# Last group finished on VectorE with stores from two queues, 1/std through ScalarE's Ln and Exp, a first load in two parts, and one slot's turnings in pairs

## The chip, the cores and the metric

The kernel runs on one core of a Trainium2 chip. The metric is the device time of one execution in microseconds (us). Five engines run side by side, each in the order of its own queue: TensorE (PE; its weight loads are PEld), VectorE (DVE), ScalarE (ACT), GpSimd (POOL) and SyncE (SP), which here only issues DMA transfers. ScalarE can issue transfers too. They wait for each other through semaphores.

## The reference

Attention over 8 batches, 8 heads, 576 tokens and 64 features a head, in which only scores within tau of a row's maximum count; then a layer norm and a two-layer network on the 512 features, added to its input.

```python
scores = scale * np.matmul(q, k.transpose(0, 1, 3, 2))
thresh = np.max(scores, axis=-1, keepdims=True) - tau
scores = np.where(scores >= thresh, scores, -1000000000.0)
scores = scores - np.max(scores, axis=-1, keepdims=True)
attn = np.exp(scores)
attn = attn / (np.sum(attn, axis=-1, keepdims=True) + 1e-09)
x = np.matmul(attn, v)            # heads side by side: (8, 576, 512)
mu = np.mean(x, axis=-1, keepdims=True)
var = np.mean((x - mu) ** 2, axis=-1, keepdims=True)
xn = (x - mu) / np.sqrt(var + 1e-06) * g_ln
ch = np.maximum(xn @ w_ch1, 0.0) @ w_ch2
return (x + ch).astype(np.float32)
```

All numbers are float32, apart from the network's weights, which arrive as 64-bit floats and are converted in the kernel. The norm's gain g_ln is multiplied into the first weights, and the division by the standard deviation is put off until after the second layer.

## The kernel before

**Attention in slots.** Each batch takes nine slots (SLOTS); a slot treats 256 query rows of two heads, or, in the fifth slot of a batch, the rows that are left of all heads. One loop over the 72 slots writes out the order of all instructions by hand: the program fixes each engine's queue, nothing is reordered later. In a slot TensorE makes the scores (`scores`, L408), VectorE their negated maximum (L422), GpSimd the threshold (L426), ScalarE the exponentials (L436), VectorE the masked weights and their sum (L443). In batch 0 the weights are turned by TensorE against diagonal matrices of 1/sum (`turn_weights`: four turnings `tp`, each copied out of PSUM by ScalarE at L493 or L487, and a rest `tr`); in later batches they go through VectorE transposes and a trip to DRAM (`turn_blocks`). `values_of` multiplies them by v.

**When a turning runs.** `at_quarter(n, i, fn)` puts a call off to place i of slot n. The places -3 to -1 come before the slot's exponentials are issued, the place 0 between the exponentials of the first and of the second two blocks, 1 to 3 later. For the four steps of `turn_weights` the main loop names four places in the next slot (L1090). In the first five slots these are (-1, -1, 0, 0), in the next three (-1, -1, -1, -1), in the ninth (-1, 0, 1, 2).

**The network in groups.** Sixteen groups of 288 tokens follow behind the attention, their matmuls poured between those of the slots by `second_part`. A group starts with the mean over features (`mean_of`, a matmul) and the centring on VectorE (L666, `centre`), then the first layer (`first_part`, tile p, relu at L795 on ScalarE). Within it ScalarE squares the centred input, TensorE sums it to var, ScalarE adds eps (L811), and VectorE makes 1/std in `root`: a first guess by integer arithmetic (L727) and three Newton rounds of three instructions (L731, L734, L735). Mean, var, p, the turnings and the second layer's sums take turns in two PSUM buffers of the pool ps_ff; a new tile waits until the last reader of the old one is done.

**The second layer** of groups 1 to 15 (`second_quarters`) multiplies in seven segments of quarter size (tile seg). ScalarE copies each segment's sum out of PSUM (L880); additions on VectorE and GpSimd combine them to y. `later` queues such calls, which the main loop takes out bit by bit (`drip`). `finish` (L892 and the addition L884) multiplies by 1/std and adds x, on GpSimd; "hi" is the upper half of the features (chunks m = 2 and 3), "done11" and "done12" are the lower half in two parts. `store` transposes a chunk on VectorE (L709) and `send` writes it with four transfers (L716), all issued by SP. A chunk's four transfers hold 32 features each.

**The head.** The queries and keys of the first head pair are loaded with four transfers each (`load_qk`), q issued by SP, k by ScalarE. A transfer is issued only when an earlier one that had the same semaphore has landed, so the order on these queues counts. `turn` scales q on GpSimd (L356) and transposes k and q on VectorE (L359, L368, L369). Meanwhile `constants(22)` keeps TensorE busy with 22 products of constants (88 matmuls; tile warm). ScalarE's function table is loaded where its first exponential stands.

Of the kernel before, what the change touches and what calls it, by code (L numbers as in the profile page):

```python
# [10 lines left out]
I32 = mybir.dt.int32  # L11
# [7 lines left out]
def kernel(  # L19
# [83 lines left out]
    def load_qk(u, engines=(nc.sync, nc.sync), room=None):  # L103


        b, hp = units[u]
        tiles = []
        for i, (name, src) in enumerate((("q", q), ("k", k))):
            if room is None:
                t = ins.tile([128, NB, 32], F32, tag=name, bufs=1, name=f"{name}_in")  # L110
            else:
                t = room[:, i * S : i * S + S].rearrange("p (n c) -> p n c", c=32)
            for h in range(2):
                for e in range(2):
                    g = 2 * h + e
                    engines[i].dma_start(
                        out=t[32 * g : 32 * g + 32],
                        in_=src[b, 2 * hp + h, :, 32 * e : 32 * e + 32].rearrange(
                            "(r n) c -> r n c" if i and b else "(n r) c -> r n c", r=32
                        ),  # L120
                    )
            tiles.append(t)
        loaded[u] = tuple(tiles)

    def load_v(u):
        b, hp = units[u]
        vt = ins.tile([128, 2, J, D], F32, tag="v", name="v_in")
        vr = v_rest[hp]
        both = v[b, 2 * hp : 2 * hp + 2]
        if b:  # L130
            nc.sync.dma_start(
                out=vt.rearrange("p h c d -> p h (c d)"),
                in_=both[:, : J * 128].rearrange("h (p c) d -> p h (c d)", c=J),
            )
        for h in range(0 if b else 2):
            nc.sync.dma_start(
                out=vt[:, h], in_=both[h, : J * 128].rearrange("(c p) d -> p c d", p=128)
            )
        for j in range(2):
            nc.sync.dma_start(  # L140
                out=vr[64 * j : 64 * j + 64, j], in_=both[:, J * 128 :].rearrange("h p d -> p h d")
            )
        values_in[u] = (vt, vr)
# [9 lines left out]
    for t in v_rest:  # L153
        nc.gpsimd.memset(t, 0.0)
    load_v(0)
    make_identity(nc, ident)
    nc.vector.memset(eps_sb, 1e-6)
    nc.vector.memset(avg_sb, 1.0 / DM)
# [186 lines left out]
    def turn(u):  # L345

        q_in, k_in = loaded.pop(u)
        qT = att.tile([128, 2, QH], F32, tag="qT", bufs=4, name="qT")
        kT = att.tile([128, S], F32, tag="kT", bufs=4, name="kT")
        ql = q_last[u % HP]
        nc.gpsimd.tensor_scalar(  # L356
            out=q_in, in0=q_in, scalar1=scl_sb, scalar2=1.0, op0=ALU.mult, op1=ALU.mult
        )
        nc.vector.transpose(kT, k_in.rearrange("p n c -> p (n c)"))  # L359
        for s in range(2):  # L360
            part = q_in[:, 9 * s : 9 * s + 8]
            if by_blocks(u):
                nc.vector.transpose(
                    qT[:, s].rearrange("p (j a c) -> p a j c", j=2, a=4),
                    part.rearrange("p (a j) c -> p a j c", j=2),
                )
            else:
                nc.vector.transpose(qT[:, s], part.rearrange("p n c -> p (n c)"))  # L368
        nc.vector.transpose(  # L369
            ql.rearrange("p (t c) -> p t c", t=2),  # L370
            q_in.rearrange("p (t n) c -> p t n c", t=2)[:, :, 8],
        )
        turned[u] = (qT, kT, ql)
# [338 lines left out]
    def send(g, m, ot):  # L712
        b, t = divmod(g, 2)
        for i in range(4):
            f = m * 128 + 32 * i
            nc.sync.dma_start(  # L716
                out=out[b, t * TOK : (t + 1) * TOK, f : f + 32].rearrange(
                    "(n r) c -> r n c", r=32
                ),
                in_=ot[32 * i : 32 * i + 32].rearrange("p (n c) -> p n c", c=32),  # L720
            )

    def root(y, x, t, step=0):


        if step == 0:
            nc.vector.tensor_scalar(  # L727
                out=y.bitcast(I32), in0=x.bitcast(I32), scalar1=-0.5, scalar2=float(0x5F3759DF),
                op0=ALU.mult, op1=ALU.add,
            )  # L730
        nc.vector.scalar_tensor_tensor(  # L731
            out=t, in0=y, scalar=-0.5, in1=y, op0=ALU.mult, op1=ALU.mult
        )
        nc.vector.tensor_mul(t, t, x)  # L734
        nc.vector.scalar_tensor_tensor(out=y, in0=t, scalar=1.5, in1=y, op0=ALU.add, op1=ALU.mult)  # L735
        if step == 0:
            root(y, x, t, 1)
        elif step == 1:
            aside.append(lambda: root(y, x, t, 2))
        else:  # L740
            rooted.append(y)

    rooted = []
    HT, HD, HM = TOK // 2, ND // 2, NK // 2
# [30 lines left out]
    def first_part(g):  # L775


        xc = centred.pop(g)
        rb = sq = None
        plain = g == 0  # L780
        sums_of = differences() if g == 1 else iter(())
        for d in range(ND):
            while conversion.ended < 4 * (d // 4 + 1):
                yield 0, 0
            while d == ND - 2 and len(rooted) <= g:
                run_all(aside)
            p1 = ps_ff.tile([128, TOK], F32, tag="ff", name="p1")
            for c in range(NK):
                product(
                    p1, lhsT=w1_sb[c][:, d * 128 : (d + 1) * 128], rhs=xc[:, c],  # L790
                    start=(c == 0), stop=(c == NK - 1),
                )
                if c < NK - 1:
                    yield 1, 1
            nc.scalar.activation(hidden[:, d], p1, func=AF.Relu)  # L795
            next(sums_of, None)
            yield 2, 1
            if sq is None and d and (plain or part > 1 or d == ND // 2 - 1):
                squared = d
                sq = hidden[:, ND - NK :]  # L800
                nc.scalar.activation(sq, xc, func=AF.Square)
                for c in range(1, NK):
                    nc.gpsimd.tensor_tensor(out=sq[:, 0], in0=sq[:, 0], in1=sq[:, c], op=ALU.add)
            elif sq is not None and rb is None and (
                d >= squared + (7 if plain else 3) and part > (0 if plain else 1)
                or d == ND - NK - 1
            ):
                var = ps_ff.tile([128, TOK], F32, tag="ff", name="var")
                product(var, lhsT=avg_sb, rhs=sq[:, 0], start=True, stop=True)
                rb = ffn.tile([128, TOK], F32, tag="rb", bufs=2, name="rb")  # L810
                nc.scalar.activation(sq[:, 2], var, func=AF.Identity, bias=eps_sb)  # L811
                aside.append(lambda: root(rb, sq[:, 2], sq[:, 3]))
                yield 1, 1
        for _ in sums_of:
            pass
        return rb
# [18 lines left out]
    def second_quarters(g, rb):  # L835
# [13 lines left out]
        def later(*calls, urgent=None):  # L849
            for what, cost, fn, eng, *args in calls:  # L850

                def go(what=what, fn=fn, eng=eng, args=args):
                    fn(eng, *args)
                    done.add(what)

                drops.append((urgent, now, eng, cost, go))
# [29 lines left out]
        def finish(eng, i, j=None):  # L886
# [6 lines left out]
            add(eng, z, z, x)  # L893

        dve, pool = nc.vector, nc.gpsimd
        later(("t3", 3, by_fours, pool, b12, b22, b12, ALU.subtract), urgent=pool)
        banks_taken[0] = True
        yield from segment(w2[0, 0], b11, y11)
# [21 lines left out]
        later(  # L920
            ("u4", 1, add, dve, y12, y21, p5), ("u3", 1, add, dve, y21, y21, p7),
            ("22", 1, add, dve, y22, y21, p5), ("21", 1, add, dve, y21, y21, p4),
            ("hi", 3, finish, pool, 1),
        )
        yield 2, 0.5
        last = segment(s4, b22)
        for _ in range(12):
# [2 lines left out]
        while waiting_mean:  # L930
            mean_of(waiting_mean.pop(0))
        p3 = yield from last
        later(("12", 1, add, dve, y12, y12, p3), ("done12", 2, finish, pool, 0, 1))
        later(*((f"o{m}", 1, store, dve, g, m, y[:, m]) for m in (2, 3, 0, 1)))
        yield 2, 0.5

    def ffn_steps(g):
# [99 lines left out]
    for n in range(NS):  # L1037
# [46 lines left out]
        if blocks_go:  # L1084
            scr = turn_blocks(s, es)
            at_quarter(n + 1, 0, lambda s=s, scr=scr, box=box: box.append(fetch(s, scr)))
        else:

            made = turn_weights(s, es, diags)
            for i, at in enumerate(  # L1090
                (-1, -1, 0, 0) if s <= HP else (-1, -1, -1, -1) if s < 2 * HP else (-1, 0, 1, 2)
            ):
                if i < 3:
                    at_quarter(n + 1, at, next, made)
                else:
                    at_quarter(n + 1, at, lambda made=made, box=box: box.append(next(made)))
# [62 lines left out]
```

## Time and profile before

| what | value |
|---|---|
| median of 3 runs (lowest to highest) | 1367.26 us (1367.08 to 1368.72) |
| the profiled execution | 1367.01 us |
| its span, first to last instruction | 1365.0 us |
| granted TensorE clock | 0.997 |
| TensorE busy, share of the span | 97% |
| VectorE, ScalarE, GpSimd busy | 68%, 33%, 45% |
| first matmul; first scores; last matmul ends | 2.36; 10.17; 1352.7 us |
| last store issued; span ends | 1362.2; 1365.0 us |

A line of a timeline has start and length in us, engine, line of the kernel, operation, the tile it writes and those it reads, and in brackets how long the engine stood idle before it and what it waited for. "x4" means that four instructions are drawn together. In lists of waits the numbers are us in total, how many times, and the longest. "SPq" is a queue that issues transfers. TensorE's matmuls overlap, so its busy time shows that it has work, not how fast it is; the waits show where it has none.

### The profile page before, as it was taken

To read this page: it belongs to the slowest core of one execution; us is meant where nothing else is said; L and a number is where in the kernel's file an instruction comes from. 1 tells how busy PE (TensorE), PEld (TensorE's weight loads), DVE (VectorE), ACT (ScalarE), POOL (GpSimd) and SP (SyncE) were. 2 spreads that over 40 slices of the span, in tenths; PEclk is the share of its full clock that TensorE was granted. 3 is DMA by queue.
4 is the path that set the end of the run, shared out by engine and by line. 5 is a ranking of instruction groups with operands and counts; after the bars stand their busy time and mean duration, and the time that the engine had idled before them with its cause. 6 is when DMAs were issued, how large, how long until landed. Compare 5 with 4: busy or idle time off the path is not lost.

```text
span 1365.0 us, 40999 instructions
## 1 busy us (share of the span) xinstructions
PE 1330.1 (97%) x17648; PEld 1007.4 (74%) x17648; DVE 921.5 (68%) x1638; ACT 455.3 (33%) x991; POOL 616.7 (45%) x823
## 2 busy tenths in 40 slices
PE   8989999999999999999999999999999999999996
PEld 7766666868677686867778696877869687786966
DVE  6988967776765777676776767657776767666211
ACT  4866532232322323232333323233232223333120
POOL 3554445444534444444534554443444445344313
PEclk9999999999999999999999999999999999999998
DMA  9822475357644666437744476446754476444201
GB/s 170 248 66 88 105 198 156 140 166 196 187 149 145 183 175 193 150 119 191 203 136 162 137 202 176 149 145 187 200 167 149 138 180 179 145 151 143 53 16 18
DMA packets 322020, 206.88 MB, mean 152 GB/s; under 512 B 247984, under 2 KB 279472, under 8 KB 313776
## 3 DMA queue, kind: packets, MB, share of 16 engines
q1 hardware_dynamic: 317072, 203.68, 51.9%
q8 instruction: 138, 2.26, 0.7%
q10 hardware_dynamic: 4736, 0.59, 0.4%
q14 instruction: 42, 0.34, 0.1%
q0 software_dynamic: 32, 0.00, 0.0%
HBM read 120.46 MB, written 83.76 MB: 150 GB/s over the span
## 4 chain that ended last, share of the span: by engine, by line
PE 88%; DVE 4%; ACT 3%; POOL 1%; issue 1%; DMA 0%; POOLq 0%; DVEq 0%; ACTq 0%; SPq 0%
PE p L101 35%; PE seg L101 31%; PE sc L408 10%; PE sc L591 8%; PE sc L601 2%; PE tp L101 1%; DVE e L443 1%; ACT e L436 1%; DVE w L298 1%; PE var L101 0%; PE mean L101 0%; DMA x_room<-in_moe_w_ch_dram 0%; DVE neg L422 0%; DVE et L533 0%; DVE w L275 0%
## 5 line engine op out<-in xcount | busy, mean ns | idle before, releaser
L101 PE MATMUL p<-xc,w 128*64 128x288 f32 x4096 | 518.2, 408 | 13.0 <-ACT hidden L795 5.0
L101 PEld LDWEIGHTS p<-xc,w 128*64 128x64 f32 x4096 | 288.3, 137 | 220.6 <-issue 15.2
L422 DVE TENSOR_REDUCE neg<-sc 128x2 f32<-128x1152 f32 x144 | 188.7, 1351 | 242.5 <-PE sc L408 241.9
L459 POOL TENSOR_SCALAR e<-e,den 128x576 f32<-128x576 f32 x252 | 193.4, 779 | 134.6 <-DVE den L448 134.6
L101 PE MATMUL seg<-hidden,w 128*64 128x144 f32 x3840 | 247.9, 287 | 0.0
L101 PEld LDWEIGHTS seg<-hidden,w 128*64 128x64 f32 x3840 | 234.9, 137 | 11.5 <-issue 8.5
L443 DVE SCALAR_TENSOR_TENSOR e<-sc,thr,e 128x576 f32<-128x576 f32 x288 | 222.2, 810 | 17.9 <-POOL thr L426 11.6
L795 ACT ACTIVATE hidden<-p 128x288 f32<-128x288 f32 x256 | 106.3, 416 | 323.3 <-PE p L101 323.2
L426 POOL TENSOR_SCALAR thr<-neg,low_sb 128x2 f32<-128x2 f32 x144 | 41.5, 288 | 377.5 <-DVE neg L422 377.4
L436 ACT ACTIVATE e<-sc,neg 128x576 f32<-128x576 f32 x288 | 197.6, 754 | 4.1 <-DVE neg L422 4.1
L533 DVE STREAM_TRANSPOSE et<-e 128x1152 f32<-128x1152 f32 x112 | 153.3, 1374 | 14.3 <-POOL e L459 13.7
L408 PE MATMUL sc<-kT,qT 64*64 64x384 f32 (+3 forms) x2048 | 139.5, 404 | 1.9 <-DVE e L443 1.7
L591 PE MATMUL sc<-em,v_in 128*64 128x128 f32 (+1 forms) x2368 | 129.5, 263 | 0.0
L591 PEld LDWEIGHTS sc<-em,v_in 128*64 128x64 f32 x2368 | 122.8, 137 | 7.9
L101 PE MATMUL seg<-hidden,stage 128*64 128x144 f32 x1920 | 123.3, 287 | 0.0
L101 PEld LDWEIGHTS seg<-hidden,stage 128*64 128x64 f32 x1920 | 117.6, 137 | 2.9 <-issue 2.9
L614 ACT COPY x<-sc 128x128 f32<-128x128 f32 x120 | 31.6, 265 | 242.0 <-PE sc L408 171.5
L865 POOL TENSOR_TENSOR hidden<-hidden 128x576 f32<-128x576 f32 x60 | 84.8, 1427 | 51.9 <-ACT hidden L795 42.3
L408 PEld LDWEIGHTS sc<-kT,qT 64*64 64x64 f32 x2048 | 76.3, 133 | 42.6 <-issue 21.0
L880 ACT COPY part<-seg 128x288 f32<-128x288 f32 x75 | 30.2, 403 | 194.2 <-PE seg L101 190.2
L865 DVE TENSOR_TENSOR hidden<-hidden 128x576 f32<-128x576 f32 x60 | 51.2, 887 | 49.1 <-PE seg L101 46.1
L101 PE MATMUL seg<-hidden,e 128*64 128x144 f32 x960 | 65.3, 286 | 0.0
(140 smaller groups left out, 1140.1 us busy)
## 6 DMA issues: line engine op xcount, KB each, us to landing
scr<-et SPq DMA_DIRECT2D x63, 1152.0 KB, 4.9
em<-scr SPq DMA_DIRECT2D x63, 1024.0 KB, 5.8
out_dram<-ot SPq DMA_DIRECT2D x256, 36.0 KB, 3.7
q_in<-in_q_dram SPq DMA_DIRECT2D x124, 72.0 KB, 2.7
k_in<-in_k_dram SPq DMA_DIRECT2D x120, 72.0 KB, 3.0
er<-scr SPq DMA_DIRECT2D x126, 64.0 KB, 5.2
v_in<-in_v_dram SPq DMA_DIRECT2D x28, 256.0 KB, 5.5
w<-in_moe_w_ch_dram SPq DMA_DIRECT2D x12, 512.0 KB, 5.0
```

The source lines that it names most:

```text
L101: nc.tensor.matmul(out[r], lhsT=lhsT[:, r], rhs=rhs, **flags)
L408: nc.tensor.matmul(sc[h][64 * i : 64 * i + 64, at : at + n], lhsT=ql[r] if s == HP else qT[r, half, j * 128 + 64 * i : j * 128 + 64 * i + 64],
L422: nc.vector.tensor_reduce(out=neg[:, i], in_=pairs[h], axis=AXL.X, op=ALU.max, negate=True,)
L426: nc.gpsimd.tensor_scalar(out=thr[:, i], in0=neg[:, i], scalar1=-1.0, scalar2=low_sb, op0=ALU.mult, op1=ALU.add,)
L436: nc.scalar.activation(es[:, i], blocks[i], func=AF.Exp, bias=neg[:, i : i + 1])
L443: nc.vector.scalar_tensor_tensor(out=es[:, i], in0=blocks[i], scalar=thr[:, i : i + 1], in1=es[:, i], op0=ALU.is_ge, op1=ALU.mult, accum_o ...
L459: nc.gpsimd.tensor_scalar(out=es[:, i], in0=es[:, i], scalar1=den[:, i : i + 1], scalar2=1.0, op0=ALU.mult, op1=ALU.mult,)
L533: nc.vector.transpose(et[:, :, 64 * h : 64 * h + 64].rearrange("p n (j c) -> p j n c", j=2), es[:, 2 * h : 2 * h + 2].rearrange("p j (n c) ...
L591: nc.tensor.matmul(dst[64 * h : 64 * h + 64], lhsT=vt[:, h, c, :], rhs=pick(em[:, 2 * j : 2 * j + 2, c], h), start=c == 0 and first, stop= ...
L614: nc.scalar.copy(x_of(2 * b + (s > HP))[:, s % (HP + 1), 128 * j : 128 * j + 128], pv[j])
L795: nc.scalar.activation(hidden[:, d], p1, func=AF.Relu)
L865: eng.tensor_tensor(out=out[at], in0=in0[at], in1=in1[at], op=op)
```

## The change

The change has four parts.

In the **last group** `finish` runs on VectorE for "hi" and "done12"; the stores of chunks 2 and 3 are queued right behind "hi" instead of behind "done12", and the second and fourth transfer of each chunk are issued by ScalarE.

**1/std**: ScalarE takes the logarithm of var + eps and exp(-0.5 times it), and VectorE makes one Newton round in place of the guess and three rounds. A table set that holds both functions is named ahead of the first activation.

**The first q** is loaded in two parts (8 and 10 of 18 row blocks), with eight transfers in place of four, and is scaled in two instructions.

**The slot's turnings**: the slot with s = 5 in batch 0 gets the places (-1, -1, 0, 0). They run in the seventh slot.

```diff
@@ load_qk
-            for h in range(2):
-                for e in range(2):
-                    g = 2 * h + e
-                    engines[i].dma_start(
-                        out=t[32 * g : 32 * g + 32],
-                        in_=src[b, 2 * hp + h, :, 32 * e : 32 * e + 32].rearrange(
...
+            for at in (slice(0, 8), slice(8, NB)) if u == 0 and i == 0 else (slice(0, NB),):
+                for h in range(2):
+                    for e in range(2):
+                        g = 2 * h + e
+                        rows = src[b, 2 * hp + h, 32 * at.start : 32 * at.stop]
+                        engines[i].dma_start(
+                            out=t[32 * g : 32 * g + 32, at],
+                            in_=rows[:, 32 * e : 32 * e + 32].rearrange(
...
     load_v(0)
+    nc.scalar.preload_act_table_set("natural_log_exp_and_others")
     make_identity(nc, ident)
@@ turn
-        nc.gpsimd.tensor_scalar(
-            out=q_in, in0=q_in, scalar1=scl_sb, scalar2=1.0, op0=ALU.mult, op1=ALU.mult
-        )
+        for at in (slice(0, 8), slice(8, NB)) if u == 0 else (slice(0, NB),):
+            nc.gpsimd.tensor_scalar(
+                out=q_in[:, at], in0=q_in[:, at], scalar1=scl_sb, scalar2=1.0,
+                op0=ALU.mult, op1=ALU.mult,
+            )
@@ send
-            nc.sync.dma_start(
+            (nc.scalar if g == NG - 1 and i % 2 else nc.sync).dma_start(
@@ root
-    def root(y, x, t, step=0):
-        if step == 0:
-            nc.vector.tensor_scalar(
-                out=y.bitcast(I32), in0=x.bitcast(I32), scalar1=-0.5, scalar2=float(0x5F3759DF),
-                op0=ALU.mult, op1=ALU.add,
-            )
+    def root(y, x, t):
         nc.vector.scalar_tensor_tensor(
             out=t, in0=y, scalar=-0.5, in1=y, op0=ALU.mult, op1=ALU.mult
         )
         nc.vector.tensor_mul(t, t, x)
         nc.vector.scalar_tensor_tensor(out=y, in0=t, scalar=1.5, in1=y, op0=ALU.add, op1=ALU.mult)
-        if step == 0:
-            root(y, x, t, 1)
-        elif step == 1:
-            aside.append(lambda: root(y, x, t, 2))
-        else:
-            rooted.append(y)
+        rooted.append(y)
@@ first_part
                 nc.scalar.activation(sq[:, 2], var, func=AF.Identity, bias=eps_sb)
+                nc.scalar.activation(rb, sq[:, 2], func=AF.Ln)
+                nc.scalar.activation(rb, rb, func=AF.Exp, scale=-0.5)
                 aside.append(lambda: root(rb, sq[:, 2], sq[:, 3]))
@@ second_quarters
+        done_by = pool if g < NG - 1 else dve
...
-            ("hi", 3, finish, pool, 1),
+            ("hi", 3, finish, done_by, 1),
         )
+        if g == NG - 1:
+            later(*((f"o{m}", 1, store, dve, g, m, y[:, m]) for m in (2, 3)))
...
-        later(("12", 1, add, dve, y12, y12, p3), ("done12", 2, finish, pool, 0, 1))
-        later(*((f"o{m}", 1, store, dve, g, m, y[:, m]) for m in (2, 3, 0, 1)))
+        later(("12", 1, add, dve, y12, y12, p3), ("done12", 2, finish, done_by, 0, 1))
+        later(
+            *((f"o{m}", 1, store, dve, g, m, y[:, m]) for m in ((2, 3, 0, 1) if g < NG - 1 else (0, 1)))
+        )
@@ main loop
-                (-1, -1, 0, 0) if s <= HP else (-1, -1, -1, -1) if s < 2 * HP else (-1, 0, 1, 2)
+                (-1, -1, 0, 0) if s <= HP + 1 else (-1, -1, -1, -1) if s < 2 * HP else (-1, 0, 1, 2)
```

More of the change, by code (lines that the diff above doesn't have):

```diff
@@ L112, in load_qk @@
                 t = room[:, i * S : i * S + S].rearrange("p (n c) -> p n c", c=32)
-            for h in range(2):
-                for e in range(2):
-                    g = 2 * h + e
-                    engines[i].dma_start(
-                        out=t[32 * g : 32 * g + 32],
-                        in_=src[b, 2 * hp + h, :, 32 * e : 32 * e + 32].rearrange(
-                            "(r n) c -> r n c" if i and b else "(n r) c -> r n c", r=32
-                        ),
-                    )
+            for at in (slice(0, 8), slice(8, NB)) if u == 0 and i == 0 else (slice(0, NB),):
[6 more added lines that the diff above has]
+                            in_=rows[:, 32 * e : 32 * e + 32].rearrange(
+                                "(r n) c -> r n c" if i and b else "(n r) c -> r n c", r=32
+                            ),
+                        )
             tiles.append(t)
@@ L721, in send @@
             )
-    def root(y, x, t, step=0):
-        if step == 0:
-            nc.vector.tensor_scalar(
-                out=y.bitcast(I32), in0=x.bitcast(I32), scalar1=-0.5, scalar2=float(0x5F3759DF),
-                op0=ALU.mult, op1=ALU.add,
-            )
+    def root(y, x, t):
         nc.vector.scalar_tensor_tensor(
@@ L932, in second_quarters @@
         p3 = yield from last
-        later(("12", 1, add, dve, y12, y12, p3), ("done12", 2, finish, pool, 0, 1))
-        later(*((f"o{m}", 1, store, dve, g, m, y[:, m]) for m in (2, 3, 0, 1)))
+        later(("12", 1, add, dve, y12, y12, p3), ("done12", 2, finish, done_by, 0, 1))
+        later(
+            *((f"o{m}", 1, store, dve, g, m, y[:, m]) for m in ((2, 3, 0, 1) if g < NG - 1 else (0, 1)))
+        )
         yield 2, 0.5
```

## The prediction

> **What bounds the kernel now.** I read the page's part 1 (busy shares), then whom TensorE waited for, then the busy time by stretches, then timelines of the stretches in which it waits.
>
> ```profile
> PE 1330.1 (97%) x17648; PEld 1007.4 (74%) x17648; DVE 921.5 (68%) x1638; ACT 455.3 (33%) x991; POOL 616.7 (45%) x823
> ...
> PE p L101 <- ACT hidden L795: 5.0, 3, 2.0
> PE p L101 <- ACT part L880: 4.6, 8, 0.6
> ...
> PE p L101 <- ACT hidden L811: 1.7, 1, 1.7
> ```
>
> TensorE is busy 1330.1 of 1365.0 us. The stretch table says where the rest lies:
>
> ```profile
> 83.00:218.00 135.00, 124.98 (x1349) 80.43 (x1349) 111.72 (x195) 67.41 (x139) 64.46 (x71) 1.00 0.42 111
> 218.00:1352.00 1134.00, 1129.08 (x15096) 864.29 (x15098) 740.74 (x1315) 332.14 (x736) 508.63 (x689) 1.00 0.53 154
> 1352.00:1365.00 13.00, 0.66 (x12) 0.39 (x8) 2.87 (x5) 0.40 (x1) 3.69 (x4) 0.67 0.28 45
> ```
>
> The first number after the stretch's length is TensorE's busy time. From 218 to 1352 it lacks 4.9 us in 1134, most of it one 0.57 us wait for the copy L880 in each batch, which the change leaves alone. So the removal of VectorE work there is worth nothing. What the change can win is in the 12.3 us after TensorE's last matmul, in the waits before 218, and in the head.
>
> **The change part by part.** Sums are made against the profiled execution: 1367.01 us, of which 1365.0 is the span and 2.0 lies around it. The median of the runs is 1367.26.
>
> *Last group's finish and stores.* The tail now (start, length):
>
> ```profile
> 1348.79 0.40 ACT L880 COPY part<-seg 128x288 f32<-128x288 f32 x1 [3.52 <-PE seg L101]
> 1349.29 1.93 DVE L884 TENSOR_TENSOR y<-y,part 128x288 f32<-128x288 f32 x4 [7.49 <-ACT part L880]
> 1351.30 1.41 POOL L892 TENSOR_TENSOR y<-y,rb 128x576 f32<-128x576 f32 x1 [6.22 <-DVE y L884]
> 1352.79 0.40 ACT L880 COPY part<-seg 128x288 f32<-128x288 f32 x1 [3.60 <-POOL y L892]
> ...
> 1353.22 1.28 DVE L884 TENSOR_TENSOR y<-y,part 128x288 f32<-128x288 f32 x1 [1.99 <-ACT part L880]
> 1354.42 0.82 DVE L709 STREAM_TRANSPOSE ot<-y 128x288 f32<-128x288 f32 x2
> ...
> 1354.92 7.78 SPq L716 DMA_DIRECT2D out_dram<-ot  x16
> ...
> L716 SPq DMA_DIRECT2D out_dram<-ot x16: 315/453/455, 1354.9 to 1362.2; - x16
> ...
> DMA to landing us min/median/max: 1.6/1.7/1.7
> ```
>
> SP issues sixteen stores without a break, about 0.5 us each; the last is issued at 1362.2, lands 1.7 later, and the end follows 1.1 after that. The issue queue sets the end. In the built changed program the order on ScalarE is: copy of p5, four stores of chunks 2 and 3, copy of p3 (the L880 that stands at 1352.79), four stores of chunks 0 and 1. A store waits for its transpose, and ScalarE takes its queue in order, so **the last copy is queued behind four stores**, and the VectorE addition of p3, the last two chunks and their stores wait for it. Worked out: additions end 1351.22. "hi" on VectorE is two instructions of 576 columns. The nearest row is L865's, 0.76 us alone: 1352.75. Two transposes at 0.41: 1353.57. ScalarE's four stores start at about 1353.25 and pace at 0.5: 1355.1. Copy 0.40: 1355.5. Addition and finish of 288 columns, three at 0.46 (the median L884 on VectorE; the 1.28 above is the same addition beside a GpSimd instruction, and GpSimd now has none there): 1356.95. Transposes: 1357.4 and 1357.8. Two queues issue four stores each from 1357.45, the last at 1358.8; 1.7 to land and 1.1 to the end: 1361.6. **The tail gains 3.4 us.** Bounds: without the block the copy stays at 1352.8, the p3 addition starts once VectorE is free at 1353.6, and everything behind is 1.9 earlier: 5.3. If two queues land no faster than one, half of the 2 us saved in issuing chunks 0 and 1 and some more goes: 2.2. The Trainium skill ("Trainium Kernel Development and Optimization", Key Constraints) speaks against the second queue: all queues run on the same 16 DMA engines, and issuing from several only saves the sequencer's issue time. By that rule a second queue brings nothing where the engines set the pace. The row decides: landing stays at 1.7 while one store is issued every 0.5, and the DMA engines are 0.3 to 0.5 busy while the stores run (the DMA view of this window), so issue time is what is short; I take the full halving.
>
> *1/std.* Seven of ten VectorE instructions a group go (L727 and two rounds of L731, L734, L735), about 3.4 us; Ln and Exp come onto ScalarE behind L811, 128x288 each. ScalarE's nearest row is L795, 0.41; both depend on the one before, so +0.87. In group 1:
>
> ```profile
> 213.37 0.45 DVE L731 SCALAR_TENSOR_TENSOR hidden<-rb 128x288 f32<-128x288 f32 x1
> 213.85 0.46 DVE L734 TENSOR_TENSOR hidden<-hidden 128x288 f32<-128x288 f32 x1
> 214.35 0.46 DVE L735 SCALAR_TENSOR_TENSOR rb<-hidden,rb 128x288 f32<-128x288 f32 x1
> 214.72 2.62 DVE L422 TENSOR_REDUCE neg<-sc 128x2 f32<-128x1152 f32 x2
> ...
> 217.52 0.42 ACT L795 ACTIVATE hidden<-p 128x288 f32<-128x288 f32 x1
> ...
> 218.00 1.19 PE L101 MATMUL p<-xc,w 128*64 128x288 f32 x8 [1.97 <-ACT hidden L795]
> ```
>
> The maximum (L422) stands behind the root; the exponentials wait for it, the relu L795 stands behind them, and TensorE waits for the relu. The scores are there at 211.9. With 3.4 us less on VectorE the maximum starts at 211.95, the relu ends at about 215.4, before TensorE wants it (215.9). The stall goes, 2.1 us against the usual 0.24 between matmuls. **−2.1.** What is late next is TensorE itself. In group 0 it is the other way: ScalarE works without a gap from L811 at 117.28 to the relu at 121.49, for which TensorE waits (next matmul at 122.02). Ln and Exp stand in that chain: **+0.85**. VectorE's root there now waits for Exp (118.65 instead of 117.89), with the weight conversion L298 behind it, but is 7 instructions shorter; that also clears the 0.48 us wait at 158.13, whose maximum started 2.3 us behind its scores: **−0.5**. In the other 14 groups ScalarE is idle for 1.5 to 1.6 us behind L811 (287.83: next relu at 289.94), which covers 0.87; without that cover it would cost up to 0.87 a group. Tables: the trace has one load, 1.28 us at 8.35; the Trainium skill ("ScalarE: Activation LUTs", Table sets and What ACT_TABLE_LOAD costs) says that a change of set costs 2.66 us and that one set holds both Ln and Exp. The built program has one load too, behind the same eight k transfers, with 4 us of cover before the first exponential at 13.77: 0, where two sets would cost two loads a group (a rival below).
>
> *Slot seven's turnings in pairs.* Now (77.6 to 83.6): four turnings, then mean, centring, first p at 83.58. After: two turnings, mean, two turnings. Only two PSUM buffers serve turnings, mean and p. In the built order mean takes the one that the first turning frees, so the last two turnings share the other, and the fourth waits for the copy of the third, which on ScalarE now stands behind two exponentials (1.36). Worked out: second copy ends 80.24, exponentials 81.6, third copy 82.2, fourth turning 82.35 to 83.25, its copy to 84.1, p at 84.25. **+0.65** (0 to +0.9). The centring is 2.4 us earlier, but p now waits for a buffer. What follows to 122 hangs on p: relus, then a ScalarE chain without a gap.
>
> *First q in two parts.* TensorE's 88 warm-up matmuls run from 2.36 to 10.24, and the first scores start at 10.17, on their heels. An earlier qT finds TensorE busy: **0**. SP issues four more transfers ahead of unit 1's q, the v's and the first weights (issued at 13.01, about 5 us to landing, wanted at 20.08); I allow −0.2 to +0.5.
>
> **Sum:** tail −3.4; middle −2.1 +0.85 −0.5 +0.65 = −1.1; head 0. Together −4.5: a span of 1360.5, a profiled time of 1362.5, and against the median **1362.8 us**.
>
> **The rivals.** (1) The middle gives nothing: the stall at 218 goes, but slot seven, Ln and Exp and a late load take all of it. For it: TensorE is what is late next, by 0.4 us only. 1367.26 − 3.4 = 1363.9. (2) The copy of p3 is not held by the stores. For it: 5.3 is the tail without the block; against it: the built order. 1367.26 − 5.3 − 1.1 = 1360.9. (3) Slower: Ln and Exp change table sets in each group. By the row two loads are 2.56, with 0.87 for the work 3.4, against 1.6 of idle time on ScalarE and about 1.3 more until TensorE needs the next relu: 0.5 a group, 16 groups, +8, less the 4.5: 1371. By the skill's 2.66 a switch, 3.3 a group: +53, 1415. It decides from the first group in which a second load appears, as soon as loads and work pass 2.9 us. Against it: a single load in the built order. (4) The change does what it says, but part of it is behind cover anyway: that is q in the forecast already.
>
> **How the numbers follow.** Chances: forecast 0.57, (1) 0.20, (2) 0.16, (3) 0.05, other 0.02. About 0.2%, 2.7 us, is what a measurement tells from no change, so "faster" is below 1364.5. The forecast is faster in nearly all its range, (2) always, (1) in somewhat over half: 0.82; "same" takes the rest of (1) and the edge of the forecast, 0.13; slower 0.05. Range: the low end takes 5.3 in the tail and 1.8 in the middle, 1360.2; the high end 2.2 and nothing, 1365.1.
>
> **What would show it.** No wait of TensorE for a relu near 217. Ln and Exp of about 0.4 us behind each L811, and in group 0 a wait near 123. First p about 0.6 us later against the scores before it. Scores still at 10.2. In the tail the last copy behind ScalarE's stores, near 1354; TensorE's end near 1351.6, and 9 us from there to the end instead of 12.3. A copy that starts as TensorE ends makes (2) right; more than one table load makes (3) right; TensorE ending after 1353 makes the middle wrong.

## The result and the profile after

The changed kernel takes **1362.86 us** (median of 7 runs, 1362.33 to 1363.47); the kernel before took 1367.08 in the runs made beside it (1366.81 to 1368.72). The ratio is 0.9966, with a 95% interval of 0.9954 to 0.9977: 4.2 us less, clear of the noise. Two of the seven executions of the kernel before, and five of the ten of the tail alone below, whose median so lies between two groups, took about 1.7 us longer than the rest (there at a granted clock 0.001 lower; the last section comes back to it). The profiled execution took 1362.91 us with a span of 1361.1: 3.9 us less span than before, and 0.2 less around it. The forecast was 1362.8.

The line numbers below are those of each profiled kernel; an edit moves them by a few. First the page's busy shares and the longest rows of the list of waits of the changed kernel (total us, times, longest):

```profile
PE 1329.7 (98%) x17648; PEld 1005.7 (74%) x17648; DVE 873.6 (64%) x1530; ACT 469.9 (35%) x1023; POOL 614.2 (45%) x820
```

```profile
PE p L101 <- ACT part L877: 4.6, 8, 0.6
PE p L101 <- ACT hidden L790: 4.1, 3, 1.5
...
PE p L101 <- ACT hidden L806: 1.7, 1, 1.7
```

VectorE has 48 us less to do, and that alone bought nothing: the eight waits of 0.57 us in the steady part (L880 before, L877 here) are the same 4.6 us in total. Of the three waits for a relu (L790) the longest is now 1.5 where it was 2.0. The table by stretches (first number after the length: TensorE busy) has the same stretch from 218 as before:

```profile
83.00:218.00 135.00, 126.31 (x1364) 80.51 (x1362) 102.71 (x178) 70.54 (x146) 65.30 (x71) 1.00 0.42 111
218.00:1352.00 1134.00, 1128.38 (x15096) 863.32 (x15092) 699.73 (x1218) 343.65 (x761) 508.52 (x687) 1.00 0.52 154
```

From 218 on TensorE is as busy as before (the last 0.7 us of the stretch now lie behind its end). So the span's 3.9 us lie before 218 and in the tail. By positions in the two traces they divide as follows (minus is a gain):

| place | predicted | measured |
|---|---|---|
| start of the scores (10.17 → 9.72) | 0 | −0.45 |
| slot seven: first turning to first p (5.94 → 6.22) | +0.65 | +0.28 |
| Ln and Exp in group 0, waits at 122 | +0.85 | +0.90 |
| wait at 158 | −0.5 | 0 |
| wait at 216 to 218 | −2.1 | −2.15 |
| end of the last matmul to end of the span (12.35 → 9.8) | −3.4 | −2.5 |

**The stall at 216 is gone.** VectorE, then ScalarE, in the changed kernel:

```profile
211.38 0.46 DVE L735 SCALAR_TENSOR_TENSOR rb<-hidden,rb 128x288 f32<-128x288 f32 x1
211.75 0.69 DVE L767 TENSOR_TENSOR stage<-w 128x512 f32<-128x512 f32 x1
212.84 2.62 DVE L427 TENSOR_REDUCE neg<-sc 128x2 f32<-128x1152 f32 x2 [0.40 <-PE sc L413]
```

```profile
215.65 0.42 ACT L790 ACTIVATE hidden<-p 128x288 f32<-128x288 f32 x1
```

Before, the maximum started at 214.72 with the scores there since 212. Now it waits for the scores (0.40, "PE sc"); the relu comes at 215.65 instead of 217.52, and TensorE runs through.

**The tail.** ScalarE, VectorE and SP's queue:

```profile
1352.03 1.92 ACTq L721 DMA_DIRECT2D out_dram<-ot  x4
1354.06 0.40 ACT L877 COPY part<-seg 128x288 f32<-128x288 f32 x1 [6.21 <-DMA out_dram<-ot]
1356.54 1.91 ACTq L721 DMA_DIRECT2D out_dram<-ot  x4
```

```profile
1351.52 0.84 DVE L714 STREAM_TRANSPOSE ot<-y 128x288 f32<-128x288 f32 x2
1354.49 0.46 DVE L881 TENSOR_TENSOR y<-y,part 128x288 f32<-128x288 f32 x1 [2.14 <-ACT part L877]
...
1356.03 0.84 DVE L714 STREAM_TRANSPOSE ot<-y 128x288 f32<-128x288 f32 x2
```

```profile
1352.02 6.34 SPq L721 DMA_DIRECT2D out_dram<-ot  x8
```

TensorE ended at 1351.33. The last copy starts 2.7 us later: ScalarE's four stores, which stand ahead of it, wait for their transposes until 1352.03 and then take 1.92 us in all. VectorE, which needs the copy, stands idle for 2.14; both queues pause with it (SP's 6.34 us hold only eight stores).

### The profile page after: what moved, and what is told of

It reads as the page before. It is cut to its first block, busy times and chain, and to the rows that moved or that the text cites. A ratio compares the mean times of both kernels' runs of the same rounds, so it can differ in the third digit from the quotient of the medians.

```text
span 1361.1 us, 40915 instructions
## 1 busy us (share of the span) xinstructions
PE 1329.7 (98%) x17648; PEld 1005.7 (74%) x17648; DVE 873.6 (64%) x1530; ACT 469.9 (35%) x1023; POOL 614.2 (45%) x820
## 4 chain that ended last, share of the span: by engine, by line
PE 89%; DVE 4%; ACT 3%; POOL 1%; issue 1%; DMA 0%; ACTq 0%; DVEq 0%; POOLq 0%; SPq 0%
PE p L101 36%; PE seg L101 30%; PE sc L413 10%; PE sc L596 8%; PE sc L606 2%; PE tp L101 1%; DVE e L448 1%; ACT e L441 1%; DVE w L301 1%; PE var L101 1%; PE mean L101 0%; DMA x_room<-in_moe_w_ch_dram 0%; ACT em L498 0%; DVE w L278 0%; ACT part L877 0%
## 5 line engine op out<-in xcount | busy, mean ns | idle before, releaser
L790 ACT ACTIVATE hidden<-p 128x288 f32<-128x288 f32 x256 | 106.4, 416 | 309.1 <-PE p L101 309.1
L877 ACT COPY part<-seg 128x288 f32<-128x288 f32 x75 | 30.3, 403 | 196.7 <-PE seg L101 190.0
```

## Experiments

**Parts alone, on the kernel before.** First the two with the least effect. Slot seven:

```diff
-                (-1, -1, 0, 0) if s <= HP else (-1, -1, -1, -1) if s < 2 * HP else (-1, 0, 1, 2)
+                (-1, -1, 0, 0) if s <= HP + 1 else (-1, -1, -1, -1) if s < 2 * HP else (-1, 0, 1, 2)
```

> Kernel before with only slot seven's turnings in pairs. Theory: the first p comes 0.28 us later after the start of the turnings than before (6.22 instead of 5.94 us), with a TensorE wait of about 0.7 before the fourth turning, and centring some 2.5 us earlier; the shift stays: about 1367.6. Rival: the wait at 216 to 218 in the kernel before takes it up, because the maximum there is late by VectorE's own chain: 1367.3, no difference after 218.

One execution: 1367.03 us, the kernel before beside it 1367.04. The time doesn't tell, the trace does: the first p comes 6.21 us after the first turning (77.53 to 83.74), the wait at 216 stays at 1.97, and the last matmul ends 0.22 later than before, although the scores began 0.13 earlier. So **the part costs about 0.3 us**, and the stall does not take it up. TensorE in the changed kernel at that place:

```profile
77.21 1.97 PE L101 MATMUL tp<-diag,e 128*64 128x128 f32 x32
79.08 0.71 PE L101 MATMUL mean<-sum,avg_sb 128*64 128x288 f32 x4
79.87 1.09 PE L101 MATMUL tp<-diag,e 128*64 128x128 f32 x16
81.65 1.09 PE L101 MATMUL tp<-diag,e 128*64 128x128 f32 x16 [0.69 <-ACT em L498]
```

The fourth turning waits for ScalarE's copy of the third, which stands behind two exponentials. The mean comes earlier, but p is not earlier for it.

First q in two parts (the edits of `load_qk` and `turn`):

```diff
+            for at in (slice(0, 8), slice(8, NB)) if u == 0 and i == 0 else (slice(0, NB),):
...
+        for at in (slice(0, 8), slice(8, NB)) if u == 0 else (slice(0, NB),):
```

> Kernel before with only the first q in two parts. Theory: the scores begin when both the warm-up matmuls and the first half of qT are done; the warm-up ends at a time that depends on when the matmul pace changes from 0.21 to 0.11 us a pair (8.33 us before, 7.33 after), which the q split does not set. So the start of the scores lies on the heels of the warm-up, at 9.7 with an early change of pace and at 10.2 with a late one, and qT's halves are ready by 8.7. Rival: the split alone brings the 0.45 us, then the scores start at 9.7 whatever the pace does. Time within 0.6 us of the kernel before.

1367.07 against 1367.04, one execution each. The scores began at 10.19, on the heels of the warm-up, with qT's halves ready by 8.8. Then for its time:

> The first q in two parts alone once more, now for its time. Theory: the warm-up's end varies from run to run between 8.8 and 10.2, the kernel before cannot start its scores before 10.04 where q is ready, and this one starts where the warm-up ends; so the median falls by 0.2 to 0.6 us: 1366.6. Rival: the early start is lost again behind unit 2's loads in all runs: 1367.05.

1366.89 us (1366.55 to 1370.73, 11 runs) against 1366.99; ratio 0.9999 (0.9990 to 1.0008): **no effect that can be measured**. The lower median that I expected is not shown. Why the trace of the changed kernel has a gain there all the same is seen in the starts of the warm-up's matmuls: a pair takes 0.21 us at first and 0.11 later, and the moment of the change differs from run to run. (Matmuls overlap: scores "on the heels" of the warm-up start 0.07 before its modelled end.)

| kernel | q | pace changes at | warm-up ends | scores start |
|---|---|---|---|---|
| before | whole | 8.33 | 10.24 | 10.17 |
| slot seven alone | whole | 5.59 | 8.92 | 10.04, waits for q |
| tail alone | whole | 6.26 | 9.27 | 10.04, waits for q |
| q alone, first | parts | 8.35 | 10.26 | 10.19 |
| q alone, again | parts | 7.54 | 9.89 | 9.82 |
| changed | parts | 7.33 | 9.79 | 9.72 |
| root later (below) | parts | 5.41 | 8.86 | 8.79 |

With q whole, the scores never start before 10.04. With q in parts and 22 products, they start where the warm-up ends. TensorE of slot seven alone, then of root later:

```profile
6.46 2.46 PE L101 MATMUL warm<-ident,avg_sb 128*64 128x128 f32 x42
10.04 2.17 PE L408 MATMUL sc<-kT,qT 64*64 64x384 f32 x32 [1.12 <-DVE qT L368]
```

```profile
7.82 1.04 PE L101 MATMUL warm<-ident,avg_sb 128*64 128x128 f32 x16
8.79 2.17 PE L413 MATMUL sc<-kT,qT 64*64 64x384 f32 x32
```

A shorter warm-up, on both kernels, one execution each:

```diff
-    constants(22)
+    constants(12)
```

> Kernel before with 12 instead of 22 warm-up products (48 instead of 88 matmuls). Warm-up ends at about 7.6 us. If q is what is late before (qT's halves at about 10.0 and 10.3), the scores still start at 10.0 to 10.2 and nothing is won; TensorE then waits 2.5 us for qT. If only the warm-up held the scores, they start before 9.7. If the pause lowers the clock, the 32 score matmuls take more than the 2.17 us that they took before.

> Changed kernel with 12 instead of 22 warm-up products. qT's first half is ready at about 8.3 and q_last at 8.8. Theory: the q split is hidden behind the warm-up, so with less of it the scores start at 8.4 to 8.8, about 1.0 us earlier than the 9.72 of the changed kernel, and 0.9 to 1.3 us of that stay to the end. Rival: the clock is not up by then and the scores take about 4 us instead of 2.17, or what follows waits for unit 1's loads: no gain.

On the kernel before: 1370.96 us, 3.9 slower. TensorE waited 3.44 us for q, and then the clock was down (the number before the last two of a stretch is the granted clock):

```profile
6.60:10.04 3.44, 0.00 (x1) 0.00 (x0) 1.27 (x3) 1.28 (x1) 0.74 (x1) 0.80 1.53 140
10.04:14.09 4.05, 4.05 (x32) 1.76 (x33) 0.40 (x2) 0.00 (x0) 0.00 (x0) 0.50 1.11 181
```

The 32 score matmuls took 4.12 instead of 2.17. That makes 1.8 of the 3.9 us. About 1.7 more come much later, where TensorE waits 1.97 us for the relu (217.9 to 219.9 here) and the clock falls once more:

```profile
216.90:220.30 3.40, 1.43 (x14) 0.62 (x12) 3.40 (x4) 2.30 (x5) 1.94 (x3) 1.00 0.93 295
220.30:223.70 3.40, 3.40 (x18) 1.71 (x16) 3.33 (x11) 1.12 (x4) 1.65 (x3) 0.50 0.46 96
```

On the changed kernel the scores began at 8.19, 1.53 earlier than with 22 products, at full pace; but the time was 1362.96, and the first turning of slot seven came at 77.13, only 0.08 earlier. VectorE shows what took it:

```profile
24.80 0.78 DVE L364 STREAM_TRANSPOSE kT<-k_in 128x576 f32<-128x576 f32 x1 [1.97 <-DMA k_in<-in_k_dram]
```

Unit 2's k landed at 24.68 (24.01 in the changed kernel), behind the first weights, and VectorE waited 1.97 us for it. The lead over the changed kernel, 1.53 us until then, is down to 0.09 us within the scores that need this k (at 31.6). **The load of unit 2 is the next bound**, close behind the present one.

**The two parts that gain.** The tail alone:

```diff
+        done_by = pool if g < NG - 1 else dve
...
-            ("hi", 3, finish, pool, 1),
+            ("hi", 3, finish, done_by, 1),
...
+            (nc.scalar if g == NG - 1 and i % 2 else nc.sync).dma_start(
```

> Kernel before with only the tail's part of the change. Theory: TensorE's last matmul ends where it did (1352.7, give or take 0.15 for the start of the scores), the last copy stands behind ScalarE's first four stores and starts about 2.6 us after it, and from the end of the matmuls to the end of the span it is 9.8 us instead of 12.4: 2.5 us less, 1364.6 us. Rival: the tail's gain hangs on the middle too (VectorE's shorter chain in the last group), then less than 2 us. The 3.4 us of the prediction would give 1363.7.

1364.84 us (1363.92 to 1365.64, 10 runs), ratio 0.9977 (0.9968 to 0.9986). ScalarE in the profiled execution of 1363.93:

```profile
1353.35 1.92 ACTq L716 DMA_DIRECT2D out_dram<-ot  x4
1355.38 0.40 ACT L880 COPY part<-seg 128x288 f32<-128x288 f32 x1 [6.21 <-DMA out_dram<-ot]
```

The last matmul ended at 1352.64, so the last copy starts 2.7 us after it here too. From the last matmul to the end of the span it is 9.5 us (9.8 in the changed kernel): 2.5 to 2.85 us less than before, without help from the middle, so the rival falls. Of the 0.3 between the two, 0.25 lies behind the landing of the last store (0.90 us to the end here, 1.15 there).

1/std alone (Ln, Exp and one Newton step):

```diff
+                nc.scalar.activation(rb, sq[:, 2], func=AF.Ln)
+                nc.scalar.activation(rb, rb, func=AF.Exp, scale=-0.5)
```

> Kernel before with only Ln, Exp and one Newton step. Theory: the TensorE wait of 1.97 us at 216 goes (2.1 less), the wait at 122 grows from 0.25 to 1.0 and group 0's second relu comes 0.9 later, and the waits at 154 to 183 stay as they are: last matmul at 1351.4, time 1365.9. As the prediction had it, the wait of 0.48 at 158.13 would go too: 1365.4. Rival: Ln and Exp cost something in the other 14 groups, then more waits than eight of 0.57 between 267 and 1292.

1365.55 us (1365.29 to 1365.90, 10 runs), ratio 0.9987 (0.9977 to 0.9996). Its waits between 100 and 1300 us:

```profile
PE p L101 <- ACT part L873: 4.6, 8, 0.6
PE p L101 <- ACT hidden L802: 1.7, 1, 1.7
PE tp L101 <- ACT em L494: 1.2, 2, 0.7
PE p L101 <- ACT hidden L786: 1.0, 1, 1.0
```

One wait for a relu is left, 1.00 at 121.9, and none at 216. The turnings still wait 1.2 in all: 0.69, and 0.51 at 159, where the prediction had none. The last matmul ended at 1351.44, as expected. No group after the first pays for Ln and Exp: the steady waits are eight, as before.

**Undoing two costs, on the changed kernel.** The last copy ahead of ScalarE's stores of chunks 2 and 3 (`go` issues one store on the engine named; `held` keeps four of them until p3 is copied):

```diff
...
+            if g < NG - 1 or i % 2 == 0:
+                go(nc.sync)
+            elif m < 2:
+                go(nc.scalar)
+            else:
+                held.append(go)
...
         p3 = yield from last
+        while held:
+            held.pop(0)(nc.scalar)
```

> Changed kernel, but ScalarE issues its four stores of chunks 2 and 3 behind the last copy instead of ahead of it. Theory: the four stores hold the copy for 2.6 us in the changed kernel, so it now starts within 0.2 us of the last matmul; VectorE's p3 addition follows at about 1352.4, the last transposes end at 1354.7, the last store is issued at 1356.0 and lands 2.0 later: 2.0 to 2.3 us less, 1360.7. Rival: the DMA engines, 0.9 busy while the two queues ran, set the end, because the same 16 stores now come closer together; then landings grow to 3 us or more and less than 1 us is won.

1360.02 us (1359.87 to 1362.85, 4 runs), ratio 0.9943 (0.9926 to 0.9960). The profiled execution was the one of 1362.85, in which the clock fell early on (see the end); its tail is as in the others that follow. ScalarE there:

```profile
1353.71 0.40 ACT L885 COPY part<-seg 128x288 f32<-128x288 f32 x1 [3.60 <-PE seg L101]
1354.29 4.16 ACTq L722 DMA_DIRECT2D out_dram<-ot  x8
```

The copy starts 0.1 us after the last matmul (1353.6) and delays no store: the transposes are not ready before 1354.2. From the last matmul to the end it is 7.5 us instead of 9.8. **The block behind the stores cost 2.3 us.** (The medians of the two kernels are 2.84 apart; what lies outside the tail was not traced in a run of 1360.) The DMA engines were as busy as in the changed kernel, for longer at a stretch (share in tenths, 40 slices from 1351.0 to 1361.1; the last row has the median time to landing):

```profile
DMA  0000000000000000489998898589998897000000
...
out_dram<-ot ACTq DMA_DIRECT2D x8, 36.0 KB, 2.0
```

Landing took 2.0 us as in the changed kernel: the rival falls, the engines do not set the end yet.

Ln, Exp and the Newton step of group 0 two quarters later (`stds` holds these three; `plain` is true for group 0 alone):

```diff
...
+                if plain:
+                    aside.append(lambda: aside.append(stds))
+                else:
+                    stds()
```

> Changed kernel, but in group 0 alone Ln, Exp and the Newton step are issued two quarters later, behind the relu for which TensorE waits at 122. Theory: Ln and Exp in group 0's chain on ScalarE are all of the 0.9 us there; the wait falls from 0.99 to about 0.25, the last matmul ends at 1350.5 instead of 1351.3 and 0.77 to 0.9 us are won: 1362.0. Rival: the wait comes back later as another (the Newton step then stands in front of VectorE's work on the weights at 126 or the maximum at 131): less than 0.3 us.

1361.88 us (1361.28 to 1362.54, 4 runs), ratio 0.9957 (0.9942 to 0.9972). TensorE around the wait, in the changed kernel and in this one:

```profile
117.70 4.10 PE L101 MATMUL p<-xc,w 128*64 128x288 f32 x32 [1.74 <-ACT hidden L806]
122.80 1.44 PE L101 MATMUL p<-xc,w 128*64 128x288 f32 x10 [0.99 <-ACT hidden L790]
```

```profile
117.02 6.83 PE L101 MATMUL p<-xc,w 128*64 128x288 f32 x52 [1.75 <-ACT hidden L806]
```

The wait of 0.99 is gone and does not come back: between 80 and 153 this kernel gained 0.89 us on the changed one. (It was 0.70 ahead before that, from scores that started at 8.79; of 0.93 us won at the start, 0.23 was lost by 77.) So **Ln and Exp in group 0's chain are all of the 0.9**, and nothing needs 1/std so early.

**Together.** The two edits, and slot seven's turnings as before:

> Changed kernel with three edits together: the last copy ahead of ScalarE's stores, group 0's Ln and Exp two quarters later, and slot seven's turnings as they were before. If the three are independent, 2.3 + 0.9 + 0.3 = 3.5 us less than the changed kernel: 1359.4. If one hides another (slot seven's 0.28 reappears as a longer wait at 116, where TensorE waits for ScalarE anyway), 1359.7.

**1358.79 us** (1358.58 to 1359.80, 5 runs), ratio 0.9939 (0.9925 to 0.9952). The last matmul ends at 1349.5 and 7.5 us follow. Against the trace of the changed kernel: start of the scores −0.6, slot seven −0.28, group 0 −0.88, tail −2.33. Each edit brings what it brought alone, so they are independent; the −0.6 belongs to no edit but to an early change of pace, and accounts for what this execution is below the 1359.4 expected.

Then the third weight transfer behind unit 2's q and k, with 22 and with 14 warm-up products:

```diff
-        conversion.fetch(3)
+        conversion.fetch(2)
...
-            conversion.fetch(2)
+            conversion.fetch(2 if n else 3)
```

> The three edits, and the third of the first weight transfers issued behind unit 2's q and k instead of ahead of them. Theory: with the scores started before 9, the next bound is unit 2's k, which lands at 24.0 to 24.7 behind that transfer; it now lands 0.5 to 1 us earlier, TensorE's wait of 0.9 us before the scores near 30 goes, and 0.3 to 0.7 us is won over the three edits where the scores start early: 1358.9. Rival: the third weight tile is late for its conversion instead: no gain or a loss of up to 1 us.

> The same with 14 warm-up products instead of 22. The scores start at 8.2 to 8.8 in every run, whatever the pace of the warm-up does. If unit 2's k is no longer the bound, 0.5 us less than with 22 on the average: 1358.4; if it still is, no gain; if the clock is not up when the scores start, up to 2 us more.

1358.61 us (1358.51 to 1359.50), ratio 0.9936 (0.9923 to 0.9948), and 1358.40 us (1357.84 to 1358.58), ratio 0.9932 (0.9919 to 0.9944). The medians differ from 1358.79 by 0.2 and 0.4, which is less than the spread of the runs of each, so neither edit is shown to gain. In the traces: with 14 products the scores start at 8.29, 0.72 before those with 22, and 0.41 of it is left at slot seven. Whether the transfer's place matters stays open: without it, in the profiled execution of the three edits (scores at 9.13), TensorE did not wait for unit 2 at all; with 14 products VectorE still waits 0.84 us for unit 2's k.

## Why the prediction came out right

The total was right: −4.5 forecast, −3.9 in the spans of the profiled executions and −4.1 in their times. Its mechanisms were mostly right, its steps not all: two were too hopeful, the wait at 158 by 0.5 and the tail by 0.9; two too careful, the start of the scores by 0.45 and slot seven by 0.37. That the median, 1362.86, lies 0.06 from the forecast is luck: these errors cancel in part, the kernel before measured 0.18 less beside it than in the forecast's base, and the start of the scores moves from run to run.

- **Where the gain can lie**: right. The busy share of VectorE fell from 68% to 64% with no trace of it between 218 and TensorE's end.
- **The stall at 216, −2.1**: right, −2.15, by the row named (a maximum behind the root).
- **Ln and Exp, +0.85 in group 0**: right, +0.90, and zero in the other groups. The changed trace has 0.44 and 0.45 for them.
- **"That also clears the 0.48 us wait at 158.13", −0.5: wrong.** The wait is still there (before, then after):

```profile
158.61 1.09 PE L101 MATMUL tp<-diag,e 128*64 128x128 f32 x16 [0.48 <-ACT em L493]
```

```profile
159.39 1.09 PE L101 MATMUL tp<-diag,e 128*64 128x128 f32 x16 [0.49 <-ACT em L498]
```

The failing step is that VectorE's seven saved instructions would still be saved 35 us later. In the changed kernel VectorE stands idle three times on the way:

```profile
126.17 0.69 DVE L301 SCALAR_TENSOR_TENSOR w<-w 128x512 f32<-128x512 f32 x1 [1.19 <-POOL w L292]
...
131.00 2.62 DVE L427 TENSOR_REDUCE neg<-sc 128x2 f32<-128x1152 f32 x2 [2.01 <-PE sc L413]
...
137.54 0.77 DVE L368 STREAM_TRANSPOSE qT<-q_in 128x256 f32<-128x256 f32 x2 [3.24 <-POOL q_in L360]
...
155.98 2.58 DVE L427 TENSOR_REDUCE neg<-sc 128x2 f32<-128x1152 f32 x2
```

Before, it had worked without a pause up to the maximum at 132.38, but the third of these waits was there already:

```profile
136.76 0.77 DVE L363 STREAM_TRANSPOSE qT<-q_in 128x256 f32<-128x256 f32 x2 [1.08 <-POOL q_in L356]
```

From there on VectorE does the same work in both kernels without a pause, 0.78 us later in the changed one, and TensorE has been 0.78 later since 122. The maximum starts at 155.98 in place of 155.19: against TensorE, as late as before. GpSimd's q did not come earlier, so no lead got past it; that VectorE waits for it stood in the trace of the kernel before. 1/std alone has the same three waits (1.19, 2.01, 3.23) and the same wait of TensorE (0.51).
- **Slot seven, +0.65**: mechanism right, size +0.28. The term was the copies: the third ends 4.39 us after the first turning where I had 4.56, the fourth 6.17 where I had 6.46; p starts 0.05 behind it, where I had 0.15.
- **The tail, −3.4**: mechanism right, −2.5. The terms, on the clock of before (1.33 later): ScalarE's four stores start 0.1 later and take 0.07 longer than I had; the transposes that follow let the last stores start at 1357.87, not 1357.45, and each takes about 0.5 (1358.8 becomes 1359.3); landing of the last takes 2.0, not 1.7. I took 1.7 from one queue with the DMA engines 0.3 to 0.5 busy; with two queues they are 0.9 busy (tenths, 40 slices from 1351.0 to 1361.1 of the changed kernel):

```profile
DMA  0000000489999897000000000599999896000000
```

  The Trainium skill's rule that the prediction cites ("Trainium Kernel Development and Optimization", Key Constraints), that a second queue saves only issue time, agrees with what was saved: ScalarE's last four stores are issued in 1.91 us beside SP's, and landing did not get shorter. The 0.3 us may be the limit that it names, the shared engines. That is not shown: SP's stores landed in 1.8 us at the same time, so ScalarE's queue itself may be the slower one.
- **First q, 0**: measured alone, nothing (0.9999). The reason, "an earlier qT finds TensorE busy", holds in the runs in which the pace changes late; in the changed kernel's profiled run the scores came 0.45 earlier. That is not the q split's alone: with q whole they could have started at 10.04, so 0.13 of it is the earlier end of the warm-up and up to 0.32 the split.
- **Rivals.** "The middle gives nothing" falls by 1/std alone (0.9987, interval below 1). "The copy is not held" falls by the trace, and the copy ahead of the stores shows what it would have brought. Tables: one load of 1.28 us, at 8.13; no second one.

## What to carry to other kernels

An engine that issues a transfer waits, at that place in its order, for what the transfer waits for; so a second issue queue belongs on an engine that has nothing left to do, or behind its last instruction. Time saved on an engine that is not the bound is worth something only up to that engine's next wait on another engine, so look for that wait first, in the trace before the change. And before a start is made earlier, look up what arrives next: here unit 2's k took back nearly all of 1.5 us.

## What the runs showed of the hardware

The moment at which TensorE's matmuls double their pace lay between 5.13 and 8.35 us in these runs, with the same first matmul at 2.36. The Trainium skill ("TensorE: Matmul & The Clock Gate", Part 1) says that the clock is let go after a busy window of some 3.4 us that runs freely, and so at a place that differs from run to run. The spread of 3.2 us is within one such window; the earliest change, though, came 2.77 us after the first matmul, sooner than a whole one. The granted clock in the rows doesn't show the slow pace (1.00 from 2 to 8 us in the changed kernel, where it lasts until 7.33). The change of pace moves the end of the warm-up by up to 1.4 us, more than slot seven and the first q are worth together.

The clock can also fall in short waits. In the profiled execution of the copy ahead of the stores, TensorE waited 0.96 and 0.61 us around 30, with only 0.86 us of work between:

```profile
30.00:32.20 2.20, 0.86 (x4) 0.20 (x4) 2.20 (x8) 0.00 (x0) 2.08 (x3) 1.00 0.80 94
32.20:36.00 3.80, 3.69 (x30) 1.85 (x32) 2.67 (x7) 2.40 (x6) 1.29 (x1) 0.58 0.87 205
```

The granted clock is 0.58 in the next 3.8 us; 28 score matmuls took 3.67 us instead of 2.16. In the trace's record the clock is at half from 32.80 to 36.21, for 3.41 us. On the kernel before with 12 warm-up products it is at half from 8.68 to 15.51, for 6.83, and from 220.31 to 223.72, again for 3.41. For a fall the same part of the page gives an idle window of about 3.4 us. The length agrees with the record; but TensorE was not idle throughout in the 3.41 us ahead of these three falls, it was busy for 1.83, 1.33 and 1.43 of them. Nor is that a threshold: the waits of 0.86 and 0.61 around 30 in the changed kernel with 12 warm-up products did not lower the clock, nor did the wait of about 2 us at 216 in the traces of the kernel before and of q alone. What decides was not tried.

That execution's 1362.85 us, against 1359.87 to 1360.04 in the other three, fits with its fall: by slot seven it is 2.25 us behind the changed kernel, although its scores started 0.90 before. A stretch of 3.41 us at half the clock costs 1.7 us (an estimate, half its length). By so much the longer executions of the kernel before stand apart: 12 of its 34 in the experiments with several executions, and five of ten of the tail alone, but none of the ten of 1/std alone and none of the seven of the changed kernel, which have lost the wait at 216. So 1/std may also take away a fall of the clock at that wait, in some executions; it is not shown, as no longer execution of these was profiled.
